# Long filter's rows by a transposing load through DRAM, slice 6's kv by four residues, a second buffer of turned h

## The chip, the cores and the metric

The kernel runs on one NeuronCore of a Trainium2 chip. The metric is the time of one execution in device microseconds; smaller is better. The engines are TensorE (PE; its weight loads are PEld), VectorE (DVE), ScalarE (ACT), GpSimd (POOL) and SyncE (SP). SP, ACT and POOL each have a queue from which they issue DMAs, in the order in which the instructions stand there.

## The reference

A forward pass and its gradients with respect to nine inputs, for a sequence of 2048 steps and 1024 channels:

```python
xn = _layernorm(q)
k_shift = sum over 4 taps of the shifted k * shift_k      # 4-tap causal filter per channel
kv = k_shift * v
y = irfft(rfft(kv padded to 4096) * rfft(ssm_k padded to 4096))[:2048]   # long convolution
s = xn * (y + kv * ssm_D)
g = silu(((xn @ w_gate) * (xn @ w_up)) @ w_down)          # 1024 -> 3584 -> 1024
out = q + s * g
```

The outputs are `out` and the gradients of q, k, v, shift_k, ssm_k, ssm_D, w_gate, w_up and w_down. `ssm_k` is stored with channels as rows (1024 x 2048): this is the long filter, called h in the kernel. The change touches how its rows get into the layout in which the convolution reads them.

## The kernel before, in words

**Work and stages.** The 1024 channels are cut into 8 slices of 128 (`ds`), the sequence into 16 blocks of 128 (`NB`), the hidden width 3584 into 14 slabs of 256 columns (`NSL`). The kernel goes through stages in one program: layer norm and the first gate/up units; gate/up matmuls of slabs 2 to 13 with the forward convolution woven in; the down projection with the gate; the gradients of h and of the weights with the backward convolution woven in; the gradient of x.

**Gate/up stage.** `gu_unit` takes a slab and a group of four sequence blocks: per block eight 512-column matmuls (L671) into a bank of `psg` (two banks), a copy out by ScalarE (L673) into `gut`, and per group a store of `gut` to GUd on ACT's queue. VectorE multiplies the two halves (hN); TensorE later turns hN (`turn`, `turn_pair`), ScalarE copies it to hT (L705, L724), and SP's queue stores hT to HTd. The slab's weights (wslab, two buffers) are loaded by SP's queue, so slab n+2 can be loaded when slab n is done with.

**Forward convolution.** `conv_forward` is a generator that does one slice after another. For a slice it transforms h (`kind` 1) and kv (`kind` 0) to 4096 frequencies, multiplies them, and transforms back. A forward transform does matmuls into `psF` (L234, two banks), copies by ScalarE into SP tiles, and butterflies on VectorE. Two forms exist: `fwd4_half` with four residues (32 matmuls of 256 columns for a slice, few VectorE sums) and `fwd8_half` with eight (16 matmuls, more VectorE sums). The list EIGHT names the (slice, kind) pairs that take eight.

**h's rows before the change.** `load_h` loads 128 rows of ssm_k into the first half of U[5] on POOL's queue. `h_rows(ds, c)` turns one half c of them on TensorE: eight 128x128 transposes (L786, L788) into a bank, and one scaled copy by ScalarE (L789) into `hx`. It is called twice per slice. The second half of U[5] serves as a third buffer of gut for slabs 0 to 11.

**What sets the order.** `make_pump` paces the generator: each gate/up block calls `tick`, which runs the generator until the sum of its yielded weights reaches a fraction of F_TOTAL; `net` takes planned TensorE time off each weight. Behind that, a scheduler orders the instructions of each engine and of each queue by when it reckons them ready, except those kept in program order (`keep_in_program_order`, used for conv matmuls and VectorE's instructions). A DMA on SP's or ACT's queue gets one of eight semaphores in turn, shared by the two queues, and waits until the DMA that had this semaphore before has landed.

**Taps.** The four taps of k's filter are laid out for all partitions in Wbc (8 KB a partition, whole kernel long), read by `shift` in the forward stage and by `dk_units` in the last.

Of the kernel before, what the change touches and what calls it, by code (L numbers as in the profile page):

```python
# [19 lines left out]
def build_kernel(  # L20
# [11 lines left out]
    nc = tc.nc  # L32
# [74 lines left out]
    HFd = dram.tile([8, P, 16, 256], BF16, name="HFd")  # L107
    KFd = dram.tile([8, P, 16, 256], BF16, name="KFd")
    DYFd = dram.tile([8, P, 16, 256], BF16, name="DYFd")
    GUd = dram.tile([NSL, 2, P, 2, 8, SLW], BF16, name="GUd")  # L110
    Hd = dram.tile([NSL, P, 2, NB, P], BF16, name="Hd")
    HTd = [[dram.tile([4, P, n, 256], BF16, name=f"HTd{i}{j}") for j, n in enumerate((8, 8, 8, 4))] for i in range(2)]
# [12 lines left out]
    nc.scalar.activation(warm[:], warm[:], ACT.Sqrt)  # L125
    RSTD = const.tile([P, NB], F32, name="RSTD")
    RSTN = const.tile([P, NB], F32, name="RSTN")
    Wbc = const.tile([P, 4, D], BF16, name="Wbc")

    tip = tc.alloc_tile_pool(name="tip", bufs=1)  # L130
    TI = tip.tile([P, 2, 8, 2, P], BF16, name="TI")
# [9 lines left out]
    def load_bcast(bsb):  # L141

        wrow = bsb.tile([1, D, 4], BF16, name="wrow")
        st(wrow[:].rearrange("p d j -> p (d j)"), A_shift_k.rearrange("(o d) j -> o (d j)", o=1))
        wtap = bsb.tile([1, 4, D], BF16, name="wtap")

        def turn(j):
            nc.gpsimd.tensor_copy(wtap[:, j, :], wrow[:, :, j])

        def spread():  # L150
            st(WTd.rearrange("(o x) -> o x", o=1), wtap[:].rearrange("p j d -> p (j d)"))
            st(Wbc[:].rearrange("p j d -> p (j d)"), bass.AP(WTd.tensor, WTd.offset, [[0, P], [1, 4 * D]]))
        return turn, spread

    def angles(tg):
# [87 lines left out]
    def net(w):  # L243
        w -= 0.95 * pe_us[0]
        pe_us[0] = 0.0
        return w

    def fwd4_half(x, i, wp, psp, first=None):

        pe_us[0] += 1.75  # L250
        SP = wp.tile([P, 2, 2, 512], F32, name="SP", bufs=2)
        for par in range(2):
            ps = psp.tile([P, 2, 2, 256], F32, name="psF")
            cmm(ps[:, 0], T4[par], x, (i, i + 4), first if i == 0 else None, True)
            cmm(ps[:, 1], T4[par], x, (i + 2, i + 6))
            nc.scalar.copy(out=SP[:, :, par], in_=ps[:].rearrange("p s k x -> p s (k x)"))
        return SP

    def fwd4_buf(wp):
# [27 lines left out]
    def fwd8_half(x, i, SP, psp, first=None, held=False):  # L287

        pe_us[0] += 0.87
        for j in range(2):  # L290
            r = 2 * i + j
            ps = psp.tile([P, 2, 2, 256], F32, name="psF")
            cmm(ps[:, 0], T4[0], x, (r,), first if r == 0 else None, held)
            cmm(ps[:, 1], T4[0], x, (r + 4,))
            nc.scalar.copy(out=SP[:, :, j], in_=ps[:].rearrange("p s k x -> p s (k x)"))  # L295

    def fwd8(SPs, X, W, C, ahead, late=False):

# [235 lines left out]
    Dz = kst.tile([P, D], BF16, name="Dz")  # L534
    V.memset(Dz[:], 0.0)
    krow = kst.tile([P, 2, 11, 256], BF16, name="k")
    V.memset(krow[0:1, 0, 0:3, :], 0.0)
    bsb = pool("bc_sb", 1)
    tg = pool("tg", 1)
# [115 lines left out]
    def gu_unit(sl, b0, n, w, tick):  # L655

        if n == 4:
            turn_of[0] += 1
            if turn_of[0] % 3 == 0 and sl < NSL - 2:
                gut = U[5][:, 2048:4096].rearrange("p (a i f) -> p a i f", a=2, i=4)  # L660
            else:
                gut = fg.tile([P, 2, 4, SLW], BF16, name="gut")
            hN = fg.tile([P, 2, 4, P], BF16, name="hN", bufs=3)
        else:
            gut = lnp.tile([P, 2, 2, SLW], BF16, name="gut_s", bufs=6)
            hN = lnp.tile([P, 2, 2, P], BF16, name="hN_s", bufs=6)
# [26 lines left out]
        hn[0] = multiply  # L693

        def turn_pair():
            hT = fg.tile([P, 4, 2, 2, P], BF16, name="hT", bufs=1)
            two_, mate[:] = mate[0:2], mate[2:]
            ps = tr_tile()[:].rearrange("p h b x -> p h (b x)").rearrange("p h (b u) -> p h b u", u=64)
            for qq in range(4):
                for a in range(2):  # L700
                    for i in range(2):
                        turn_halves(lambda hh: ps[:, hh, 4 * qq + 2 * a + i], two_[qq // 2][:, a, qq % 2 * 2 + i, :])
            to = HTd[b0 // 8][sl // 4][:, :, 2 * (sl % 4):2 * (sl % 4) + 2, :]
            for g in range(2):
                nc.scalar.copy(out=halves(hT[:, 2 * g:2 * g + 2].rearrange("p q a i s -> p (q a i) s")), in_=ps[:, :, 8 * g:8 * g + 8])  # L705
            ht_st[0] = ld(to.rearrange("q f a s -> f q (a s)"), hT[:].rearrange("f q a i s -> f q (a i s)"))

        def store(hT):
            half, rest = divmod(b0, 8)
# [5 lines left out]
                ht_st[0] = ld(to[q0, :, :, i0 * P:(i0 + n) * P], hT[:, 0, :, 0:n].rearrange("f a i s -> f a (i s)"))  # L715

        def turn():
            hT = fg.tile([P, 4, 2, 2, P], BF16, name="hT", bufs=1)[:, 0:2] if chunk[0] > 5 else lnp.tile([P, 2, 2, 2, P], BF16, name="hT_s", bufs=5)[:]
# [10 lines left out]
    h_out = []  # L729
    cv_gone = []  # L730
    ht_st = [None]
    EIGHT = ((0, 0), (0, 1), (6, 0), (7, 0), (7, 1))
    INV8 = (2, 4, 5, 6, 7)
    SHIFT_W = 8 * 2.3

# [4 lines left out]
    def conv_forward():  # L740
        S_ = conv_state

        def load_kv(dp, c):
            S_["k", dp] = krow
            if dp > 0 or c == 0:
                for i in range(2) if dp == 0 else (c,):
                    cld_k(krow[:, i], i, dp)
            if dp > 0 or c == 1:
                for i in range(2) if dp == 0 else (c,):
                    v = U[4][:, 2048 * i:2048 * i + 2048].rearrange("p (a x) -> p a x", a=8)  # L750
                    cld_v(v, i, dp * 256, 256)

        def load_h(ds):
            hrow = U[5][:, 0:2048].rearrange("p (c u r) -> p c u r", c=2, r=8)
            cld(U[5][:, 0:2048], A_ssm_k[ds * P:(ds + 1) * P, :])
            S_["h", ds] = hrow

        def shift(dp):
            kv = cx.tile([P, NB, 256], BF16, name="kv")
            S_["kvt", dp] = kv  # L760
            k = S_.pop(("k", dp))
            wb = lambda j: Wbc[:, j:j + 1, dp * 256:(dp + 1) * 256].unsqueeze(1).to_broadcast([P, 2, 8, 256])
# [12 lines left out]
            yield 2.3  # L775

        def h_rows(ds, c):
            if ds == 8:
                return
            hrow = S_["h", ds]  # L780
            if c == 0:
                S_["hx"] = cf.tile([P, NB, P], BF16, name="hx")
# [3 lines left out]
                nc.tensor.transpose(ps[:, 0, :], hrow[:, c, :, 0], ident[:])  # L786
            for r in range(1, 8):
                nc.tensor.transpose(ps[:, r, :], hrow[:, c, :, r], ident[:])  # L788
            nc.scalar.activation(S_["hx"][:, 8 * c:8 * c + 8, :], ps, ACT.Copy, scale=WSC)  # L789
            if c == 1:  # L790
                h_out.append(ds)
                if ds + 1 < 8:
                    load_h(ds + 1)

        def kvs(ds):
            return S_["kvt", ds // 2][:, :, ds % 2 * P:(ds % 2 + 1) * P]
# [70 lines left out]
        for ds in range(8):  # L867
            yield 0.5
            if ds % 2 == 1 and ds < 7:
                with tc.issue_after(S_["kst"].ins):  # L870
                    for c in range(2):
                        load_kv(ds // 2 + 1, c)
            D0 = Dz[:, ds * P:(ds + 1) * P]
            sph = []
            KX = cx.tile([P, 16, 256], BF16, name="KX")
# [5 lines left out]
            else:  # L881
                yield from transform(ds, 0, sp, KX, own_room(HX), lambda i: sph.append(half(ds, S_["hx"], i, D0)), nop)
                S_["kst"] = st(KFd[ds], KX[:])
            calls = []

            def behind():
                calls.append(0)
                if len(calls) % 2 == 0:
                    next(tl, None)
            room = cf.tile([P, 4, 256], F32, name="room", tag="hx")[:] if eight else None  # L890
            yield from transform(ds, int(ds > 0), sph, HX if ds else KX, room, nop1 if eight else lambda c: h_rows(ds + 1, c),
                                 behind)
            if ds == 0:
                S_["kst"] = st(KFd[0], KX[:])
            if eight:
                h_rows(ds + 1, 0)
            turned(HX, 1, 0, 1)
            yield 1.3
            if eight:
                h_rows(ds + 1, 1)  # L900
            if ds == 7:
                cf.release()
                S_["filters"] = False
# [43 lines left out]
    for i, (b0, n, x4) in enumerate(xs):  # L947
# [16 lines left out]
        if i == 4:  # L964
            with tc.issue_after(act_copy[0].ins):
                nc.scalar.activation(Dz[0:1, :], Dz[0:1, :], ACT.Copy, scale=WSC)
# [237 lines left out]
    def dk_units(ew):  # L1204
# [9 lines left out]
        def load_turned(i):  # L1214
# [7 lines left out]
                nc.sync.dma_start_transpose(out=dkT[:], in_=DKSHd[ds, c * H:c * H + H, :])  # L1222
            return kT, dkT

        dk = load_rows(0)
        yield 3
        for i in range(16):
            ds, c = divmod(i, 2)
            dsl = slice(ds * P, (ds + 1) * P)
            wb = lambda j: Wbc[:, j:j + 1, dsl].to_broadcast([P, 8, P])  # L1230
# [577 lines left out]
```

## Time and profile before

| | us |
|---|---|
| median of 3 runs (lowest, highest) | 1911.72 (1911.5, 1912.55) |
| the profiled execution | 1911.63 |
| its span, first to last instruction | 1909.9 |
| TensorE busy | 1899.4 |
| VectorE busy | 1549.7 |
| ScalarE busy | 636.8 |

The profile shows one execution. Busy time is the union of an engine's instructions; TensorE's matmuls overlap in their pipeline, so what a matmul costs is read from the start of one to the start of the next. A line of the timeline has start, duration, engine, line of the kernel, operation, output<-inputs, shapes and count, and in brackets an idle time before it with what ended it. "SPq", "ACTq" and "POOLq" are DMA issues on a queue; "to landing" is from the issue's start until the data has arrived. In the slice digits of the page the gate/up stage with the forward convolution is about the first 500 us.

### The profile page before, as it was taken

Reading aid. Unit: us, or ns where it says so; the run is one execution under the profiler, and the core shown is the slowest. Engines: PE = TensorE matmul, PEld = TensorE weight load, DVE = VectorE, ACT = ScalarE, POOL = GpSimd, SP = SyncE. Lnnn points to the kernel's source line nnn. Section 1 sums busy time; section 2 is a strip of 40 time slices with the busy share of each in tenths; the row PEclk is TensorE's granted clock in tenths of the full one; section 3 lists DMA queues with packets and bytes.
Section 4 is the critical chain, followed back from the end, with each engine's and each line's share of the span. In section 5 each row is a group of like instructions: output and inputs, shape, how many; then the busy total and the mean of one; then the engine's idle time right before and its main releaser. Section 6 shows DMA issues by size and latency. Waiting matters only on the chain.

```text
span 1909.9 us, 28150 instructions
## 1 busy us (share of the span) xinstructions
PE 1899.4 (99%) x11379; PEld 1013.9 (53%) x11379; DVE 1549.7 (81%) x1711; ACT 636.8 (33%) x927; POOL 332.7 (17%) x465
## 2 busy tenths in 40 slices
PE   8999999999999999999999999999999999999999
PEld 5555555545444466666666665664444444444444
DVE  8999999999988556887999999999995305788862
ACT  5765555556333233432222222222222102111121
POOL 5121211201113220001031221211212101111120
PEclk9999999999999999999999999999999999999999
DMA  9777766769769997677897798585887999989852
GB/s 298 269 263 233 251 208 223 252 211 311 241 227 307 316 314 231 209 231 233 264 277 247 231 266 258 184 286 180 230 238 181 219 206 190 194 187 190 194 166 88
DMA packets 425106, 444.34 MB, mean 233 GB/s; under 512 B 268400, under 2 KB 342796, under 8 KB 410512
## 3 DMA queue, kind: packets, MB, share of 16 engines
q1 hardware_dynamic: 367504, 239.03, 45.9%
q0 software_dynamic: 41152, 174.15, 29.0%
q10 hardware_dynamic: 16320, 29.36, 4.1%
q8 instruction: 89, 1.46, 0.3%
q14 instruction: 41, 0.34, 0.1%
HBM read 193.87 MB, written 189.84 MB: 201 GB/s over the span
## 4 chain that ended last, share of the span: by engine, by line
PE 97%; DVE 1%; ACT 1%; DMA 0%; issue 0%; SPq 0%; ACTq 0%
PE psb L1499 20%; PE psx L1644 20%; PE psg L671 19%; PE psb L1482 10%; PE psbm L1034 10%; PE psb L1582 9%; PE psF L234 3%; PE psI L455 1%; PE tr L565 1%; PE psY L1193 1%; PE psY L445 1%; PE psx L1582 1%; DVE bst L578 0%; DMA wslab<-in_B_w_gate_dram 0%; PE tr L788 0%; DVE U L212 0%
## 5 line engine op out<-in xcount | busy, mean ns | idle before, releaser
L671 PE MATMUL psg<-wslab,U 128*128 128x512 bf16 x1792 | 401.8, 379 | 3.5 <-DMA wslab<-in_B_w_gate_dram 2.1
L1499 PE MATMUL psb<-U,U 128*128 128x512 bf16 x1792 | 397.1, 379 | 0.0
L1644 PE MATMUL psx<-U,dgut 128*128 128x512 bf16 x1536 | 332.8, 379 | 0.0
L1644 PEld LDWEIGHTS <-dgut 128*128 128x128 bf16 x1792 | 175.3, 98 | 211.4
L1499 PEld LDWEIGHTS <-U 128*128 128x128 bf16 x1792 | 175.2, 98 | 198.0
L671 PEld LDWEIGHTS <-U 128*128 128x128 bf16 x1792 | 172.6, 98 | 197.2 <-issue 3.6
L1482 PE MATMUL psb<-wdt,U 128*128 128x256 bf16 x1792 | 205.6, 273 | 0.0
L1482 PEld LDWEIGHTS <-U 128*128 128x128 bf16 x1792 | 175.2, 98 | 29.2
L212 DVE TENSOR_TENSOR W<-W 128x1024 f32<-128x1024 f32 (+1 forms) x189 | 186.5, 1003 | 4.1
L1582 PE MATMUL psb<-U,U 128*128 128x512 bf16 x816 | 177.3, 379 | 0.0
L1504 ACT CAST wb<-psb 128x512 bf16<-128x512 f32 x112 | 65.6, 586 | 315.4 <-PE psb L1499 310.5
L1249 DVE SCALAR_TENSOR_TENSOR dkp<-dkT,kT 128x1024 bf16<-128x1024 bf16 (+2 forms) x64 | 78.3, 1223 | 93.1 <-DMA dkT<-DKSHd 91.4
L1034 PE MATMUL psbm<-U,ht 128*128 128x512 bf16 x672 | 146.0, 379 | 0.0
L1582 PEld LDWEIGHTS <-U 128*128 128x128 bf16 x896 | 87.4, 98 | 104.4
L673 ACT CAST gut<-psg 128x512 bf16<-128x512 f32 x156 | 91.5, 589 | 120.2 <-PE psg L671 119.7
L1676 ACT ACTIVATE dx_t<-dxn 128x1024 bf16<-128x1024 f32 x15 | 15.9, 1057 | 324.7 <-DVE dxn L212 324.7
L1034 PEld LDWEIGHTS <-ht 128*128 128x128 bf16 x672 | 65.7, 98 | 78.1
L212 DVE TENSOR_TENSOR U<-U,dht 128x2048 bf16<-128x2048 bf16 x56 | 68.3, 1220 | 46.5 <-ACT dht L1484 46.5
L1484 ACT CAST dht<-psb 128x512 bf16<-128x512 f32 x112 | 65.6, 587 | 116.4 <-PE psb L1482 116.4
L66 POOL DMA_DIRECT2D Hd<-hN x54 | 36.6, 677 | 268.9 <-DVE hN L212 258.9
L1623 ACT CAST wbs<-psb 128x512 bf16<-128x512 f32 x51 | 29.9, 586 | 145.4 <-PE psb L1582 134.3
L212 DVE TENSOR_TENSOR W<-SP 128x1024 f32<-128x1024 f32 x64 | 74.1, 1218 | 1.3 <-ACT SP L295 0.8
(263 smaller groups left out, 2342.9 us busy)
## 6 DMA issues: line engine op xcount, KB each, us to landing
U<-GUd SPq DMA_DIRECT2D x28, 1024.0 KB, 9.3
DGd<-U SPq DMA_DIRECT2D x28, 1024.0 KB, 5.8
GUd<-gut ACTq DMA_DIRECT2D x39, 512.0 KB, 5.2
out_dram<-wb SPq DMA_DIRECT2D x112, 128.0 KB, 4.8
U<-Hd SPq DMA_DIRECT2D x14, 1024.0 KB, 6.6
Hd<-hN POOLq DMA_DIRECT2D x54, 256.0 KB, 4.5
HTd<-hT SPq DMA_DIRECT2D x24, 512.0 KB, 3.7
ht<-HTd SPq DMA_DIRECT2D x18, 512.0 KB, 7.5
```

Of the source, the lines that this page charges most:

```text
L212: pinned(V.tensor_tensor(o, a, b, op))
L234: mm = nc.tensor.matmul(ps[:, k].rearrange("p (c d) -> p c d", c=2), T[:, r, k, :], xr[:, r], start=(n == 0), stop=(n == len(rs) - 1 and ( ...
L671: gu_mm[0] = nc.tensor.matmul(ps[:], XNT[q][:, dc, qi * P:(qi + 1) * P], w[:, dc].rearrange("p a f -> p (a f)"), start=(dc == 0), stop=(dc ...
L673: nc.scalar.copy(out=gut[:, :, i], in_=ps[:].rearrange("p (a f) -> p a f", a=2))
L1034: mm = nc.tensor.matmul(ps[:, dh * 512:(dh + 1) * 512], ht(fc)[:, i * P:(i + 1) * P], WD[fc // 4][:, fc % 4, dh * 512:(dh + 1) * 512], sta ...
L1249: ins = V.scalar_tensor_tensor(prod[:].rearrange("p r d -> p (r d)")[:, lo:H], dkT[:, 0, lo:H], 1.0, kT[:, 0, 13 + m + lo:13 + m + H], op0 ...
L1482: nc.tensor.matmul(ps[:, x * SLW:(x + 1) * SLW], DBMT[2 * hf + g][:, dc, (b % 4) * P:(b % 4 + 1) * P], wdt[:, dc, :], start=(dc == 0), sto ...
L1484: nc.scalar.copy(out=dht[:, 2 * e:2 * e + 2].rearrange("p b f -> p (b f)"), in_=ps[:])
L1499: nc.tensor.matmul(ps[:], XN[b // 4][:, b % 4, dc * P:(dc + 1) * P], dgus[b // 8][:, :, b % 8], start=(b == 0), stop=(b == NB - 1))
L1504: nc.scalar.copy(out=wb[:, dc % 2].rearrange("p a f -> p (a f)"), in_=ps[:])
L1582: nc.tensor.matmul(ps, h[:, f, b, :], DBM[b // 4][:, b % 4, dh * 512:(dh + 1) * 512], start=(b == 0), stop=(b == NB - 1))
L1644: nc.tensor.matmul(ps[:, dh * 512:(dh + 1) * 512], t[n][:, f, i * P:(i + 1) * P], WGU[n][:, f, dh * 512:(dh + 1) * 512], start=(n == 0 and ...
```

## The change

1. From slice 1 on, h's rows are turned by a transposing load on SP's queue (`turn_h`), straight from ssm_k into U[5]: the partition is then a step within a block of 128. `keep_h` stores that to HRd in DRAM in the order of the sequence (SP's queue), and `h_by_rows` loads it back into `hx` with eight consecutive steps to a partition (POOL's queue). Slice 0 keeps the TensorE way.
2. The scale WSC moves from h_rows' copy (and from Dz) into the copy of h's transform out of psF (`from_bank`).
3. (6, 0) leaves EIGHT.
4. Wbc is gone; 256-channel pieces of the taps are loaded into WB (two of them) and, in the last stage, wbk.
5. hT has two buffers; `turn_pair` stores it on ACT's queue; in slabs 12 and 13 half of krow is the third buffer of gut.
6. F_TOTAL is adapted.

```diff
-    Wbc = const.tile([P, 4, D], BF16, name="Wbc")
+    HRd = dram.tile([8, S, P], BF16, name="HRd")
+    WB = kst.tile([P, 4, 2, 256], BF16, name="WB")
...
+    def from_bank(out, ps, first):
+        if first is None:
+            nc.scalar.copy(out=out, in_=ps)
+        else:
+            nc.scalar.activation(out, ps, ACT.Copy, scale=WSC)
...
-            if turn_of[0] % 3 == 0 and sl < NSL - 2:
+            if turn_of[0] % 3 == 0 and sl >= NSL - 2:
+                gut = krow[:].rearrange("p a b d -> p (a b d)")[:, 2048:4096].rearrange("p (a i f) -> p a i f", a=2, i=4)
+            elif turn_of[0] % 3 == 0:
                 gut = U[5][:, 2048:4096].rearrange("p (a i f) -> p a i f", a=2, i=4)
...
         def turn_pair():
-            hT = fg.tile([P, 4, 2, 2, P], BF16, name="hT", bufs=1)
+            hT = fg.tile([P, 4, 2, 2, P], BF16, name="hT", bufs=2)
...
-            ht_st[0] = ld(to.rearrange("q f a s -> f q (a s)"), hT[:].rearrange("f q a i s -> f q (a i s)"))
+            ht_st[0] = sta(to.rearrange("q f a s -> f q (a s)"), hT[:].rearrange("f q a i s -> f q (a i s)"))
...
-    EIGHT = ((0, 0), (0, 1), (6, 0), (7, 0), (7, 1))
+    EIGHT = ((0, 0), (0, 1), (7, 0), (7, 1))
...
+        def turn_h(ds):
+            if ds < 8:
+                nc.sync.dma_start_transpose(out=U[5][:, 0:2048].rearrange("p (j d) -> p j d", d=P),
+                                            in_=A_ssm_k[ds * P:(ds + 1) * P, :])
+
+        def keep_h(ds):
+            if ds < 8:
+                ld(HRd[ds].rearrange("(j p) d -> p j d", p=P), U[5][:, 0:2048].rearrange("p (j d) -> p j d", d=P))
+
+        def h_by_rows(ds):
+            if ds < 8:
+                S_["hx"] = cf.tile([P, NB, P], BF16, name="hx")
+                cld(S_["hx"][:].rearrange("u (c r) d -> u c (r d)", c=2), HRd[ds].rearrange("(c u r) d -> u c (r d)", c=2, u=P))
+                h_out.append(ds)
...
         for ds in range(8):
             yield 0.5
...
+            turn_h(ds + 1)
...
+            keep_h(ds + 1)
...
-            yield from transform(ds, int(ds > 0), sph, HX if ds else KX, room, nop1 if eight else lambda c: h_rows(ds + 1, c),
-                                 behind)
+            yield from transform(ds, int(ds > 0), sph, HX if ds else KX, room, nop1, behind)
+            h_by_rows(ds + 1)
...
-            if eight:
-                h_rows(ds + 1, 0)
             turned(HX, 1, 0, 1)
             yield 1.3
-            if eight:
-                h_rows(ds + 1, 1)
...
+    F_TOTAL += 0.95 * 7 * 0.95
```

More of the change, by code (lines that the diff above doesn't have):

```diff
@@ L151, in spread @@
             st(WTd.rearrange("(o x) -> o x", o=1), wtap[:].rearrange("p j d -> p (j d)"))
-            st(Wbc[:].rearrange("p j d -> p (j d)"), bass.AP(WTd.tensor, WTd.offset, [[0, P], [1, 4 * D]]))
+            load_taps(WB[:].rearrange("p j e d -> p j (e d)"), 0, 512, ld)
         return turn, spread
@@ L255, in fwd4_half @@
             cmm(ps[:, 1], T4[par], x, (i + 2, i + 6))
-            nc.scalar.copy(out=SP[:, :, par], in_=ps[:].rearrange("p s k x -> p s (k x)"))
+            from_bank(SP[:, :, par], ps[:].rearrange("p s k x -> p s (k x)"), first)
         return SP
@@ L294, in fwd8_half @@
             cmm(ps[:, 1], T4[0], x, (r + 4,))
-            nc.scalar.copy(out=SP[:, :, j], in_=ps[:].rearrange("p s k x -> p s (k x)"))
+            from_bank(SP[:, :, j], ps[:].rearrange("p s k x -> p s (k x)"), first)
     def fwd8(SPs, X, W, C, ahead, late=False):
@@ L536, in build_kernel, with load_taps @@
     krow = kst.tile([P, 2, 11, 256], BF16, name="k")
+    WB = kst.tile([P, 4, 2, 256], BF16, name="WB")
+    def load_taps(t, d0, w, queue=st):
+        queue(t, bass.AP(WTd.tensor, WTd.offset + d0, [[0, P], [D, 4], [1, w]]))
     V.memset(krow[0:1, 0, 0:3, :], 0.0)
@@ L717, in turn @@
         def turn():
-            hT = fg.tile([P, 4, 2, 2, P], BF16, name="hT", bufs=1)[:, 0:2] if chunk[0] > 5 else lnp.tile([P, 2, 2, 2, P], BF16, name="hT_s", bufs=5)[:]
+            hT = fg.tile([P, 4, 2, 2, P], BF16, name="hT", bufs=2)[:, 0:2] if chunk[0] > 5 else lnp.tile([P, 2, 2, 2, P], BF16, name="hT_s", bufs=5)[:]
             ps = tr_tile()[:, 0].rearrange("p (q a i) x -> p q a i x", q=2, a=2)
@@ L744, in load_kv @@
             S_["k", dp] = krow
+            if dp > 1 and c == 0:
+                load_taps(WB[:, :, dp % 2], dp * 256, 256)
             if dp > 0 or c == 0:
@@ L753, in load_h @@
         def load_h(ds):
-            hrow = U[5][:, 0:2048].rearrange("p (c u r) -> p c u r", c=2, r=8)
             cld(U[5][:, 0:2048], A_ssm_k[ds * P:(ds + 1) * P, :])
-            S_["h", ds] = hrow
+            S_["h", ds] = U[5][:, 0:2048].rearrange("p (c u r) -> p c u r", c=2, r=8)
+        def turn_h(ds):
[10 more added lines that the diff above has]
+                h_out.append(ds)
         def shift(dp):
@@ L761, in shift @@
             k = S_.pop(("k", dp))
-            wb = lambda j: Wbc[:, j:j + 1, dp * 256:(dp + 1) * 256].unsqueeze(1).to_broadcast([P, 2, 8, 256])
+            wb = lambda j: WB[:, j:j + 1, dp % 2].unsqueeze(1).to_broadcast([P, 2, 8, 256])
             room = cx.tile([P, 16, 256], BF16, name="KX")[:].rearrange("p a x -> p (a x)") if dp == 0 else U[7][:]
@@ L777, in h_rows @@
         def h_rows(ds, c):
-            if ds == 8:
-                return
             hrow = S_["h", ds]
@@ L788, in h_rows @@
                 nc.tensor.transpose(ps[:, r, :], hrow[:, c, :, r], ident[:])
-            nc.scalar.activation(S_["hx"][:, 8 * c:8 * c + 8, :], ps, ACT.Copy, scale=WSC)
+            nc.scalar.copy(out=S_["hx"][:, 8 * c:8 * c + 8, :], in_=ps)
             if c == 1:
                 h_out.append(ds)
-                if ds + 1 < 8:
-                    load_h(ds + 1)
         def kvs(ds):
@@ L963, in build_kernel @@
                     next(conv)
-        if i == 4:
-            with tc.issue_after(act_copy[0].ins):
-                nc.scalar.activation(Dz[0:1, :], Dz[0:1, :], ACT.Copy, scale=WSC)
         for i_, sl in ([(0, 0)], [(1, 0), (0, 1), (1, 1)], [(2, 0), (2, 1)], [(3, 0), (3, 1)], [(4, 0)], [(5, 0)])[i]:
@@ L1223, in load_turned @@
             return kT, dkT
+        wbk = None
         dk = load_rows(0)
@@ L1229, in dk_units @@
             dsl = slice(ds * P, (ds + 1) * P)
-            wb = lambda j: Wbc[:, j:j + 1, dsl].to_broadcast([P, 8, P])
+            if i % 4 == 0:
+                wbk = ew.tile([P, 4, 256], BF16, name="wbk", bufs=2)
+                load_taps(wbk[:], ds * P, 256)
+            wb = lambda j: wbk[:, j:j + 1, ds % 2 * P:(ds % 2 + 1) * P].to_broadcast([P, 8, P])
             acc = ew.tile([P, 8, P], BF16, name="dka")
```

## The prediction

> **What bounds the kernel now.** I read the page's busy times and slices first, then the busy time by stage, then the waits of TensorE.
>
> ```profile
> span 1909.9 us, 28150 instructions
> PE 1899.4 (99%) x11379; PEld 1013.9 (53%) x11379; DVE 1549.7 (81%) x1711; ACT 636.8 (33%) x927; POOL 332.7 (17%) x465
> 110.00:160.00 50.00, 50.00 (x381) 28.31 (x378) 49.13 (x43) 29.30 (x40) 12.56 (x17) 1.00 0.85 275
> 160.00:300.00 140.00, 139.41 (x997) 74.73 (x996) 137.89 (x113) 76.31 (x106) 23.92 (x34) 1.00 0.70 231
> 300.00:420.00 120.00, 120.00 (x869) 64.79 (x867) 119.03 (x105) 67.71 (x94) 21.96 (x31) 1.00 0.72 238
> PE psg L671 <- ACT gut L673: 1.1, 2, 0.9
> PE psF L234 <- DVE kv L212: 0.6, 1, 0.6
> ```
>
> The stage rows give length, then busy time of PE, PEld, DVE, ACT, POOL, the granted clock, the DMA share and GB/s. TensorE never rests after the start; VectorE is 98 to 99% full from 110 to 420 us, so it has hardly any room; ScalarE is 55 to 59% busy. The granted clock is 1.00 throughout. The last two rows (waits of TensorE) show that TensorE waits for almost nothing. So a removed TensorE instruction shortens the kernel by its own time, and any hold of TensorE lengthens it by that hold: nothing later is idle that could take it up. The executed time beside this span is 1911.63 us, 0.1 under the median of the three runs (1911.72); I work from 1911.63.
>
> **What is removed and added on TensorE.** A block of h_rows (L786, L788) is eight transposes.
>
> ```profile
> 62.99 0.22 PE L786 MATMUL tr<-ident,U 128*128 128x128 bf16 x1
> 63.05 0.60 PE L788 MATMUL tr<-ident,U 128*128 128x128 bf16 x7
> 63.48 3.62 PE L671 MATMUL psg<-wslab,U 128*128 128x512 bf16 x16
> 120.28 1.91 PE L234 MATMUL psF<-kv,TF 128*128 128x256 bf16 x16
> 122.03 3.62 PE L671 MATMUL psg<-wslab,U 128*128 128x512 bf16 x16
> ```
>
> From the first transpose's start to the next matmul's start: 63.48 - 62.99 = 0.49 us. Slices 1 to 7 have two blocks each, so 14 x 0.49 = **6.9 us go**. Slice 6's kv loses its place in EIGHT: two halves of 16 matmuls instead of two of 8, 16 more. A half of 16 takes 122.03 - 120.28 = 1.75 us: **1.75 us come**. Net on TensorE -5.15 us. (By busy time a block is 0.22 + 0.60 us, which overlaps its neighbours; by that the net would be -9.7.)
>
> **VectorE.** The same edit spares VectorE work behind the four sums that both forms share.
>
> ```profile
> 75.92 1.22 DVE L212 TENSOR_TENSOR KX<-W 128x1024 f32<-128x1024 f32 x1
> 80.72 0.68 DVE L212 TENSOR_TENSOR hN<-gut 128x1024 bf16<-128x1024 bf16 x1
> 87.72 0.69 DVE L212 TENSOR_TENSOR hN<-U 128x1024 bf16<-128x1024 bf16 x1
> 134.45 4.62 DVE L212 TENSOR_TENSOR KX<-W 128x1024 bf16<-128x1024 f32 x4
> ```
>
> Eight residues: 87.72 - 75.92 less one hN of 0.6 = 11.2 us. Four residues: 4.6 us. So VectorE is spared 6.6 us in slice 6, more than TensorE's 5.15. The planner's total also moves: F_TOTAL gains 6.3 and loses 9.5, and each slice's weight grows by the 0.9 that h_rows used to subtract, so the convolution is spread over relatively more gate/up work. TensorE thus arrives at VectorE's results at about the same absolute time; I cost this at nothing, from -1 to +5 us (all TensorE gain before slice 6 lost at waits such as the kv one above).
>
> **Small things at nothing.**
>
> ```profile
> 106.64 1.02 ACT L789 ACTIVATE hx<-tr 128x1024 bf16<-128x1024 bf16 x1 [0.26 <-PE tr L788]
> 133.09 0.38 PE L234 MATMUL psF<-hx,TF 128*128 128x256 bf16 x2
> ```
>
> ScalarE drops 14 copies and has room. The scaling that h_rows did in its copy moves into copies that exist (from_bank). Slice loads of taps, hx from HRd and wbk go to POOL's queue, and each has several us to tens of us before its use: the old hx was ready at 107.7 us and first multiplied at 133.1, and a 512 KB load takes about 6 us (the in_A_ssm_k row below). Without that cover each hx would cost its landing, 6 us. The second buffer of hT, and krow as a third buffer of gut in slabs 12 and 13, can only take waits away, and no wait on them is in the list. Behind the stage, dk's work keeps the same VectorE operations.
>
> **What moves on the queues: the term that decides.** The order of the built program (each queue's instructions with the semaphore each waits for) shows what the diff does not. The scheduler has put all seven transposing loads early. On SP, behind slab 2's load, stand T1, HRd1, an HTd store, T2, HRd2, an HTd store, slab 3, T3, an HTd store, HRd3, T4, an HTd store, HRd4, T5, HRd5, T6, HRd6, slab 4, T7, HRd7, slab 5. U[5] has one buffer for them, so T and HRd alternate: each T waits for the HRd before it to land, each HRd for its T. That is one serial chain of DMAs.
>
> Nobody needs its data soon. But eight semaphores are handed round the DMAs of SP and ACT, and each DMA waits on its queue until the previous user of its semaphore has landed. In the new order ScalarE's stores inherit semaphores of the chain. By the store's time in the profile before: GUd at 91.13 us waits for HRd2, at 99.37 for slab 3, at 108.33 for HRd3, the HTd store behind the copy of 111.75 for T4, GUd at 115.92 for HRd4, **GUd at 124.57 for T6**, at 133.91 for HRd6, at 156.50 for T7. Behind a waiting store stand ScalarE's evictions of psg and psF; TensorE has two banks of each and then stops.
>
> ```profile
> 60.00:110.00 50.00, 49.79 (x316) 27.03 (x315) 48.84 (x56) 35.15 (x45) 8.04 (x12) 1.00 0.63 212
> 645.00:1185.00 540.00, 539.88 (x3401) 331.17 (x3400) 446.33 (x473) 166.52 (x258) 90.06 (x130) 1.00 0.83 254
> 91.13 0.52 ACTq L72 DMA_DIRECT2D GUd<-gut  x1
> 99.37 0.52 ACTq L72 DMA_DIRECT2D GUd<-gut  x1
> 108.33 0.52 ACTq L72 DMA_DIRECT2D GUd<-U  x1
> 111.75 1.93 ACT L705 COPY hT<-tr 128x1024 bf16<-128x1024 bf16 x2
> 115.92 0.52 ACTq L72 DMA_DIRECT2D GUd<-gut  x1
> 124.57 0.52 ACTq L72 DMA_DIRECT2D GUd<-gut  x1
> 125.69 0.58 ACT L673 CAST U<-psg 128x512 bf16<-128x512 f32 x1 [1.14 <-PE psg L671]
> 133.91 0.52 ACTq L72 DMA_DIRECT2D GUd<-U  x1
> 156.50 0.52 ACTq L72 DMA_DIRECT2D GUd<-gut  x1
> 66.99 0.60 PE L788 MATMUL tr<-ident,U 128*128 128x128 bf16 x7
> 127.23 1.89 PE L671 MATMUL psg<-wslab,U 128*128 128x512 bf16 x8
> 129.63 1.69 PE L671 MATMUL psg<-wslab,U 128*128 128x512 bf16 x7
> L1330 SPq DMA_TRANSPOSE wdt<-in_B_w_down_dram x14: 1700/4910/12837, 644.9 to 1185.4; - x14
> DMA to landing us min/median/max: 4.2/9.3/21.7
> U<-in_A_ssm_k_dram POOLq DMA_DIRECT2D x8, 512.0 KB, 6.0
> HTd<-hT SPq DMA_DIRECT2D x24, 512.0 KB, 3.7
> YFd<-yf POOLq DMA_DIRECT2D x7, 512.0 KB, 7.9
> wslab<-in_B_w_gate_dram SPq DMA_DIRECT2D x14, 512.0 KB, 9.2
> ```
>
> T1 can start when h_rows(0) is through, 66.99 + 0.60 = 67.6 us. A T has no row of its own. The nearest is wdt: the same 512 KB turned on the same queue, landing after 4.2 to 21.7 us, median 9.3; its stretch of the kernel (645 to 1185 us) has a DMA share of 0.83, this one 0.63 up to 110 us and 0.85 after. I take 9.3. HRd writes 512 KB in pieces of 256 B: between HTd<-hT (3.7, same queue, longer pieces) and YFd<-yf (7.9, the same pieces, POOL's queue); I take 4.5, nearer to the row of its own queue. Then HRd4 has landed at 67.6 + 4 x 13.8 = 122.8, T5 at 132.1, HRd5 at 136.6. By then ScalarE is held, its stores and POOL's have stopped, so T6 gets the quiet 4.2: **140.8 us**.
>
> Held at the store of 124.57, ScalarE cannot evict (125.69). TensorE still has the unit of 127.23 for its second bank and stops ahead of the unit of 129.63; having been spared two blocks by then, it stands there at 128.6. After T6 come the store's issue, 0.52, and one eviction, 0.58: TensorE goes on at 141.9. **Hold: 13.3 us.** Everything behind it shifts by as much, so HRd6 (145.3 against 133.91 + 12.3), slab 4 (140.9 + 9.2 = 150) and T7 (154.6 against 156.5 + 12.3) come in time.
>
> Bounds of this term: with 4.2 and 3.7 throughout T6 lands at 67.6 + 6 x 4.2 + 5 x 3.7 = 111.3 and there is no hold; with 12 (inside wdt's upper half) and 5.8 it lands at 168.6 and the hold is 41.
>
> **Sum:** 1911.63 - 6.9 + 1.75 + 13.3 = **1919.8 us**, 0.4% slower.
>
> **A rule that speaks against this hold.** The Trainium skill, "Advanced Engine Details and Errata", section "X-Bar Transpose (TRN2)", states that transposing DMAs are as fast as regular ones. By it T would take the 6.0 us of the plain load of the same rows, HRd4 would land at 109.6, T6 at 67.6 + 6 x 6.0 + 5 x 4.5 = 126.1, and the sum would be the first rival's 1906.5. The trace only half agrees: wdt's quickest, 4.2, is below 6.0, its median of 9.3 well above.
>
> **Rivals.**
> 1. The chain is quick enough (faster). If T and HRd together take under 10.9 us (T6 landed by 127.5: 59.9 us for five and a half pairs), TensorE is not held: 1911.63 - 5.15 = 1906.5. For it: no one waits for the data, wdt's quiet 4.2, and the plain load's 6.0. Against: ScalarE's and POOL's stores and slab 3 share the DMA engines, and six landings in a row have to be good.
> 2. A short hold, or VectorE (no change). T6 between 129 and 136 us costs 1.5 to 9 us and eats the 5.15; or no hold comes, but VectorE, with 1 to 2% room, is where TensorE's time goes until slice 6, as at the 0.6 us wait for kv: 1908 to 1915. For it: VectorE's 98 to 99%. Against: the planner's shift and the 6.6 us spared.
> 3. A longer hold. At 12 and 5.8 us a pair the hold is 41 us, 1948; at wdt's 11 and HRd's 5 it is 67.6 + 66 + 25 - 127.5 = 31, 1938. For it: wdt's 21.7, and that from 110 us on the DMA engines are at 0.85 without the chain. Against: the hold itself stops the other traffic.
> 4. The change does not do what it says, because the loads come too late for hx. The order excludes it: all seven stand before slab 5.
>
> **How the numbers follow.** About 0.2% (3.8 us) is what a measurement of this kernel tells from no change. The forecast and the longer hold (rival 3) share the condition that T6 lands after 136.5: 0.58 together, of which the longer hold beyond 1934 is 0.08. Rival 1 has 0.24, rival 2 has 0.18. So faster 0.24, same 0.18, slower 0.58. The range reaches from rival 1's 1906 to 1934 (a hold of 27 us, T at 10.5 and HRd at 4.7), leaving out about 0.18.
>
> **What would show it.** TensorE transposes of L814 and its neighbour: 16 left. The hold: an idle time of PE psg of some ten us between 118 and 145 us, released by ScalarE's eviction, with GUd stores on ACT's queue at the landing of a transposing load; SP's queue with T and HRd in turn, T6 landing near 141. If T6 lands before 127.5 and PE has no such gap, rival 1 holds and my term is wrong in T's duration. If psF waits for kv or for the sums on VectorE between 160 and 420, it is rival 2. If the gaps sit elsewhere, at the hx loads or the slabs, my reading of the queues is wrong.

## The result and the profile after

The changed kernel takes **1944.82 us** (median of five, 1938.17 to 1947.98) against 1911.86 before (1911.5 to 1912.55): ratio **1.0169, 95% interval 1.0151 to 1.0187**. It is slower, as forecast, and by stores held behind the chain, as forecast, but by 33 us where 8 were expected; the time lies outside the range of 1906 to 1934. The profiled execution of the changed kernel is the quickest of the five, 1938.17 us (span 1936.4), so the trace below explains 26.5 us of span and not the 6.7 us by which the median is longer still.

First the page and TensorE's waits of the changed kernel (who waits for whom: us in total, times, longest).

```profile
span 1936.4 us, 27939 instructions
PE 1899.1 (98%) x11283; PEld 1009.3 (52%) x11283; DVE 1543.7 (80%) x1699; ACT 622.9 (32%) x912; POOL 337.6 (17%) x470
PE psg L683 <- ACT gut L685: 15.7, 5, 9.3
PE psg L683 <- ACT U L685: 12.3, 1, 12.3
```

TensorE now waits 15.7 + 12.3 = 28.0 us for ScalarE's evictions of psg; before, the first of these rows said 1.1. ScalarE's own timeline shows why: the stores on its queue (ACTq), with the eviction behind each.

```profile
120.27 0.54 ACTq L72 DMA_DIRECT2D GUd<-U  x1
120.93 1.07 ACT L685 CAST gut<-psg 128x512 bf16<-128x512 f32 x2 [12.11 <-DMA HRd<-U]
...
126.71 0.45 ACTq L72 DMA_DIRECT2D HTd<-hT  x1
...
132.50 0.55 ACTq L72 DMA_DIRECT2D GUd<-gut  x1
...
157.60 0.52 ACTq L72 DMA_DIRECT2D GUd<-gut  x1
158.24 0.58 ACT L685 CAST U<-psg 128x512 bf16<-128x512 f32 x1 [16.78 <-DMA U<-in_A_ssm_k_dram]
```

And the chain of waits of the same stretch (start, us, what): the transposing loads T and the stores HRd, one behind the other.

```profile
93.80 11.20 DMA U<-in_A_ssm_k_dram
105.01 15.18 DMA HRd<-U
120.21 6.42 DMA U<-in_A_ssm_k_dram
126.69 5.73 DMA HRd<-U
132.44 16.79 DMA U<-in_A_ssm_k_dram
149.24 3.82 DMA HRd<-U
153.08 4.45 DMA U<-in_A_ssm_k_dram
...
158.87 7.05 PE psg L683 x24
...
174.91 3.45 PE psg L683 x16
```

These are T3, HRd3, T4, HRd4, T5, HRd5, T6. Each store of ScalarE leaves at a landing of the chain: GUd at 120.27 behind HRd3 (120.2), HTd at 126.71 behind T4, GUd at 132.50 behind HRd4, GUd at 157.60 behind T6 (157.5). TensorE's timeline has a gap behind three of them (9.34, 3.58 and 12.26 us).

```profile
121.57 8.66 PE L683 MATMUL psg<-wslab,U 128*128 128x512 bf16 x32 [9.34 <-ACT gut L685]
133.81 2.38 PE L683 MATMUL psg<-wslab,U 128*128 128x512 bf16 x8 [3.58 <-ACT gut L685]
135.97 3.14 PE L234 MATMUL psF<-kv,TF 128*128 128x256 bf16 x16
142.40 1.91 PE L234 MATMUL psF<-kv,TF 128*128 128x256 bf16 x16
144.15 1.89 PE L683 MATMUL psg<-wslab,U 128*128 128x512 bf16 x8
158.87 6.40 PE L683 MATMUL psg<-wslab,U 128*128 128x512 bf16 x21 [12.26 <-ACT U L685]
```

Two of these rows show something else: the same 16 matmuls of psF take 3.14 us behind a gap and 1.91 us later. The table by stretch (length, then busy time of PE, PEld, DVE, ACT, POOL, the granted clock, DMA share, GB/s) says why.

```profile
100.00:120.00 20.00, 12.22 (x98) 6.21 (x97) 16.41 (x19) 4.69 (x6) 5.38 (x8) 0.86 1.02 298
120.00:130.00 10.00, 8.43 (x32) 3.48 (x32) 2.19 (x3) 4.08 (x6) 1.20 (x2) 0.76 0.72 193
150.00:160.00 10.00, 1.13 (x3) 0.40 (x3) 0.00 (x0) 1.76 (x3) 0.00 (x0) 0.50 0.66 144
160.00:165.00 5.00, 5.00 (x19) 2.06 (x18) 2.51 (x3) 4.05 (x6) 0.00 (x0) 0.76 0.99 262
```

The column before the last two is the granted clock: it falls with the gaps, to 0.50. What that costs: the 24 matmuls of 158.87 took 7.05 us, at 3.45 / 16 = 0.216 us each they take 5.2, so 1.9; the 32 of 121.57 at 0.216 plus the 0.2 that such a row counts at its end take 7.1, so 1.6; the 8 of 133.81 lose 2.38 - 1.89 = 0.5; psF loses 3.14 - 1.91 = 1.2. Together 5.2 us. The account of the profiled run closes: 28.0 - 1.1 of waits, + 5.2 of clock, - 5.15 saved on TensorE = 26.95, and the span grew by 26.5; the other waits of TensorE differ by under 1 us each.

The Trainium skill, "TensorE: Matmul & The Clock Gate", Part 1, says that TensorE falls to half its clock after an idle window of about 3.4 us and needs as long busy to leave it. The trace agrees on the half, 0.50, and about on the way back: in windows of half a us the clock is at 1.00 again 3.3 and 3.5 us after TensorE went on at 121.57 and 158.87. It fell sooner, 2.4 and 2.1 us into these two gaps.

### The profile page after: what moved, and what is told of

It reads as the page before. It is cut to its first block, busy times and chain, and to the rows that moved or that the text cites. A ratio compares the mean times of both kernels' runs of the same rounds, so it can differ in the third digit from the quotient of the medians.

```text
span 1936.4 us, 27939 instructions
## 1 busy us (share of the span) xinstructions
PE 1899.1 (98%) x11283; PEld 1009.3 (52%) x11283; DVE 1543.7 (80%) x1699; ACT 622.9 (32%) x912; POOL 337.6 (17%) x470
## 4 chain that ended last, share of the span: by engine, by line
PE 93%; DMA 5%; DVE 1%; ACT 0%; SPq 0%; issue 0%; ACTq 0%
PE psb L1523 20%; PE psx L1668 20%; PE psg L683 17%; PE psb L1506 10%; PE psbm L1054 10%; PE psb L1606 9%; PE psF L234 3%; DMA U<-in_A_ssm_k_dram 3%; DMA HRd<-U 2%; PE psI L461 1%; PE psY L1213 1%; PE tr L575 1%; PE psY L451 1%; PE psx L1606 1%; DVE bst L588 0%; DMA wslab<-in_B_w_gate_dram 0%
## 5 line engine op out<-in xcount | busy, mean ns | idle before, releaser
L683 PE MATMUL psg<-wslab,U 128*128 128x512 bf16 x1792 | 405.4, 382 | 30.4 <-ACT gut L685 15.7
L685 ACT CAST gut<-psg 128x512 bf16<-128x512 f32 x144 | 84.1, 589 | 133.3 <-PE psg L683 115.3
```

The costliest lines, as they stand in the source:

```text
L683: gu_mm[0] = nc.tensor.matmul(ps[:], XNT[q][:, dc, qi * P:(qi + 1) * P], w[:, dc].rearrange("p a f -> p (a f)"), start=(dc == 0), stop=(dc ...
L685: nc.scalar.copy(out=gut[:, :, i], in_=ps[:].rearrange("p (a f) -> p a f", a=2))
```

## The experiments

Theory 1 (the prediction's): ScalarE's stores wait for semaphores of the chain, and the evictions stand behind them. Rival A: VectorE takes the gain. Rival B: the chain's traffic itself slows TensorE's data wherever it stands. Rival C: another part of the change. "Leaves out" in an expectation tells which part of the computation is missing. The kernel before, run beside them, took 1911.85 to 1912.22 us at the median. In two kernels one execution stands far off (5204 us in the seventh, 1999 in the eighth) and nothing here explains these two; the table leaves them out.

| kernel | median us | range | ratio to before, 95% |
|---|---|---|---|
| 1 T paced by the slab loads | 1918.42 | 1911.8-1927.6 | 1.0023-1.0051 |
| 2 no chain | 1910.02 | 1906.6-1913.9 | 0.9984-1.0001 |
| 3 T without HRd | 1920.91 | 1917.8-1928.8 | 1.0039-1.0066 |
| 4 ScalarE's stores on POOL's queue | 1935.75 | 1933.1-1942.1 | 1.0116-1.0143 |
| 5 plain loads in place of T | 1920.98 | 1919.4-1923.3 | 1.0035-1.0061 |
| 6 HRd in long pieces | 1942.40 | 1938.0-1945.2 | 1.0144-1.0170 |
| 7 k and v of slices 2, 3 cut | 1927.50 | 1926.9-1929.5 | 1.0067-1.0102 |
| 8 no chain, taps early | 1914.11 | 1906.6-1919.2 | 0.9996-1.0019 |
| 9 before, (6,0) alone | 1914.07 | 1913.7-1915.4 | 0.9998-1.0015 |
| 10 no chain, HTd on SP | 1908.90 | 1906.2-1916.4 | 0.9971-0.9994 |
| 12 paced, stores on POOL | 1914.09 | 1909.3-1919.1 | 0.9996-1.0016 |

**1. Pacing.**

```
+        slab_new[0] = last            # in load_slab
+            with tc.issue_after(slab_new[0].ins):
                 nc.sync.dma_start_transpose(...)
```

> The changed kernel, but each transposing load of turn_h is set to be issued behind the newest slab load, so that on SP's queue the seven T stand one or two to a slab (T1 behind slab 2, T2 behind slab 3, T3 behind slab 5 and so on) instead of all ahead of slab 5. All data are computed as in the changed kernel. Theory (ScalarE is held because its stores wait for semaphores of a packed chain of T and HRd): no store of ScalarE waits for a T or HRd under way, the two long idle times of PE psg near 120 and 150 us are gone, the granted clock stays at 1.00, and the time is 1911.9 - 6.9 + 1.75 = 1906.7 us (1905.5 to 1909). Rival A (VectorE binds until slice 6, so the spared transposes are lost at its results): 1909 to 1912. Rival B (the transposing loads' traffic itself slows TensorE or the slabs, wherever they stand): above 1925.

1918.42 us, 26 less than the changed kernel with the same transfers: most of the loss is where T stands, not that it runs. But it is 12 above the 1906.7 expected, so theory 1 is not the whole. The profiled execution took 1913.22 us, so its trace can show only the first 6.5 us of these 12. It has one long wait in the stage, in the timelines of TensorE and ScalarE; the last row is from the median landings between 55 and 420 us.

```profile
291.24 2.29 PE L686 MATMUL psg<-wslab,U 128*128 128x512 bf16 x5 [5.43 <-ACT U L688]
267.94 0.52 ACTq L72 DMA_DIRECT2D GUd<-U  x1
290.60 1.07 ACT L688 CAST U<-psg 128x512 bf16<-128x512 f32 x2 [8.20 <-DMA GUd<-U]
U<-in_A_ssm_k_dram SPq DMA_TRANSPOSE x7, 12.9
```

A GUd store issued at 267.94, 7 us behind a T, landed at 290.5, and the eviction that needs its buffer came late. Here ScalarE waits for a store of its own to land, not for a borrowed semaphore; that much of rival B is real. The same store in the kernel without the chain (experiment 2), issued at 268.05, landed in 7.0 us.

**2. The ceiling.** turn_h and keep_h are not called; hx is loaded from in_A_ssm_k, unturned.

> The changed kernel without the transposing loads and without the stores to HRd; hx of slices 1 to 7 is loaded in the same piece size (2 KB) straight from in_A_ssm_k, unturned, so the turning of slices 1 to 7 is left out of the computation. It is the ceiling: all that the change does on TensorE, VectorE and ScalarE, without the chain. Theory: 1911.9 - 5.15 = 1906.7 us (1905.5 to 1909), no idle time of PE psg over 1 us. Rival A (VectorE takes the gain): 1909 to 1912. Rival C (the slow-down is not the chain but something else of the change, such as the taps loaded by slice, the moved HTd stores or the loads of hx): above 1925.

1910.02 us: no 28 us of waits, so the loss is the chain's (rival C falls as to size). The time would fit rival A, but the profile doesn't: its one wait on VectorE in the stage is 0.3 us, and the largest is far behind it.

```profile
PE psx L1666 <- ACT wbs L1645: 3.1, 1, 3.1
PE psF L234 <- DVE kv L212: 0.3, 1, 0.3
```

1909.9 - 5.15 + 3.1 = 1907.9, against a span of 1908.2: TensorE did gain its 5.15, and a wait in the last stage took most of it back. That this wait comes and goes would fit the range of 1906.6 to 1913.9, but one execution was profiled, so it is not shown.

**3. T alone.** keep_h is not called; T stays; hx is loaded as in kernel 2.

> As the kernel without the chain, but the seven transposing loads are kept (nobody uses their data; the stores to HRd are left out, and hx is loaded unturned, so the ordering of the rows of slices 1 to 7 is left out of the computation). The T stand early and close together on SP's queue; ScalarE's GUd store of 91 us now waits for T5 and that of 108 us for slab 3. Theory: the hold depends on what a store of ScalarE waits for, so TensorE stands once, ahead of 110 us, until T5 has landed: T1 at 67.6, five times some 8 us, so till about 108: a hold of 5 to 15 us, and 1912 to 1922 in all. If the T are as quick as the plain load of the same rows (6 us) T5 lands at 98 and the time is 1907 to 1910: then HRd alone makes the loss. If a transposing load is slowed by whatever runs beside it to 12 or more, it is above 1925 without any HRd.

The hold moved to the store that waits for T5, as the order says (ScalarE's and TensorE's timelines):

```profile
100.20 0.54 ACTq L72 DMA_DIRECT2D GUd<-gut  x1
100.78 1.86 ACT L193 COPY TI<-psT 128x2048 bf16<-128x2048 bf16 x1 [9.39 <-DMA U<-in_A_ssm_k_dram]
103.19 8.40 PE L683 MATMUL psg<-wslab,U 128*128 128x512 bf16 x31 [7.63 <-ACT gut L685]
```

T1 to T5 ran from 67.9 to 100.2, one in 6.5 us: with no HRd between them T is near a plain load's 6.0. (T7, issued at 111.1, took 20.5, with no HRd in this kernel at all; SP's next load of slab 4 left at 131.58, when T7 landed.) A hold of 7.6 us in another place, behind another link, is what theory 1 foretold and rivals A, B and C did not.

**4. The stores off ScalarE's queue.** sta issues on POOL's queue.

> The changed kernel with the GUd and HTd stores that ScalarE issues (sta) put on POOL's queue; the packed chain of T and HRd stays early on SP. All data are computed. Theory (the loss is ScalarE's evictions standing behind stores that wait for the chain): ScalarE no longer stands behind a waiting store; TensorE goes on through 115 to 160 us, except for what a late slab 4 (still behind T6 on SP) or POOL's own queue costs; 1907 to 1920. Rival B (the traffic of the chain itself, or data that come late because of it): PE psg still idles about 28 us and the time stays at 1935 to 1948.

A miss: 1935.75, where theory 1 gave 1907 to 1920. ScalarE no longer holds TensorE as it did, but the chain's other victim comes forward (SP's and TensorE's timelines):

```profile
144.75 4.41 SPq L773 DMA_TRANSPOSE U<-in_A_ssm_k_dram  x1
156.94 3.24 SPq L557 DMA_DIRECT2D wslab<-in_B_w_up_dram  x1
174.77 12.77 PE L683 MATMUL psg<-wslab,U 128*128 128x512 bf16 x47 [12.43 <-DMA wslab<-in_B_w_gate_dram]
```

Slab 4 stands behind T6 and HRd6 on SP's queue, goes out at 156.94 and keeps TensorE 12.43 us. (A further gap, 4.67 us ahead of 138.99, stands behind a copy of ScalarE that waited 5.66 us for a store of HTd to land.) So theory 1 has to be widened: the chain packed early delays **everything queued behind it or sharing its semaphores**, and freeing one victim lets the next set the end.

**5, 6, 7. What made the chain long.**

```
5 -  nc.sync.dma_start_transpose(out=U[5]..., in_=A_ssm_k[...])
  +  ld(U[5][:, 0:2048], A_ssm_k[ds * P:(ds + 1) * P, :])
6 -  ld(HRd[ds].rearrange("(j p) d -> p j d", p=P), ...)
  +  ld(HRd[ds].rearrange("(p j) d -> p (j d)", p=P), U[5][:, 0:2048])
7 k: t[u:u+n, a:] -> t[u:u+n, a:a+1]; v: a:a+4 -> a:a+1, for slices 2 and 3
```

> The changed kernel with each transposing load T replaced by a plain load of the same 512 KB on the same queue and at the same place, so that the chain of load, HRd, load, HRd keeps its order and the stores of ScalarE that wait for it stay the same (the turning of slices 1 to 7 is left out of the computation). If the transposing form is what makes the chain long (9.0 us in the mean for T1 to T6): the plain load takes about 6.0, HRd 4.5 to 6, the sixth load lands at 126 to 134 and the time is 1907 to 1918. If the chain is slow because any transfer beside so much traffic is (HRd in plain pieces took 15.2 us once): loads of 8 to 9 us, the sixth landing at 145 to 158, and 1928 to 1948.

> The changed kernel with HRd stored in one piece of 4 KB a partition instead of 16 of 256 B (the rows of slices 1 to 7 are then not put in order; that part of the computation is left out). The scheduler puts T7 ahead of slab 4 too here. If HRd's 7.2 us in the mean comes from its short pieces: HRd about 3.7, T6 lands near 140, and with the hold some 15 us shorter 1920 to 1930. If HRd waits for the traffic beside it whatever its pieces are: the sum stays at 1935 to 1950.

> The changed kernel in which the loads of k and v for slices 2 and 3 (2.4 MB on POOL's queue, issued at 110 to 133 us in the changed kernel) fetch one row of each piece only; everything else, the order of each queue and the waits included, is as in the changed kernel (the filter of slices 2 and 3 is computed from stale rows). Theory (the chain stretched in the hold because POOL's loads, already issued, shared the DMA engines with it: HRd3 15.2 and T5 16.8 us): HRd3 about 7 and T5 about 9, T6 lands near 141 instead of 157.5, the idle time of PE psg is 12 to 15 us instead of 28, and the time is 1919 to 1926, near the 1919.8 of the prediction. Rival (the transposing load itself is that slow at times, or KFd's and HFd's stores do it): 1935 to 1948.

With plain loads the sixth landed at 139.2 and the time is 1920.98, between the two answers: the kernel is 24 us quicker without the transposing form. From the start of each load to the start of its HRd, the six took 7.5, 3.8, 8.1, 4.3, 5.5 and 3.8 us; T1 to T6 in the changed kernel 8.2, 6.9, 11.2, 6.4, 16.8 and 4.4. But a plain store was stretched as well (SP's queue, kernel 5; HRd4, and the load that waits for its landing):

```profile
106.27 0.36 SPq L61 DMA_DIRECT2D HRd<-U  x1
126.09 0.34 SPq L61 DMA_DIRECT2D U<-in_A_ssm_k_dram  x1
127.45 3.53 PE L683 MATMUL psg<-wslab,U 128*128 128x512 bf16 x8 [9.64 <-ACT gut L685]
```

HRd4 took 19.8 us there. Long pieces shorten HRd (mean of the first five 4.9 us for 7.2) and change nothing in all: T4 and T6 then took 16.4 and 18.9, and T6 landed at 154.2. With k and v cut the time is 1927.50, between the two answers and 17 under the changed kernel. The transposing form is kept here, so the 24 of kernel 5 and these 17 are not shares of one sum. T5 and T6 took 5.7 and 5.4, with neither k nor v beside them: what is left of these loads also went out earlier in that kernel, at 110.8 to 122.7 us. T4 still took 19.2 (chain of waits, kernel 7):

```profile
106.82 19.20 DMA U<-in_A_ssm_k_dram
126.08 5.49 DMA HRd<-U
131.59 5.73 DMA U<-in_A_ssm_k_dram
137.33 3.81 DMA HRd<-U
141.16 5.40 DMA U<-in_A_ssm_k_dram
```

So there are two crowded places. From 105 to 125 us whatever link is under way takes 15 to 20 us, in either form and either direction: HRd3 15.2 (changed kernel), HRd4 19.8 (5), T4 16.4 (6), T4 19.2 (7). Kernel 7 shows that whole k and v are not needed for it; that it is KFd, HFd, the slab and the GUd stores that crowd it was not tried by itself. From 129 us on, in the changed kernel, it is v and k: T5 16.8 beside them, 5.7 without. Kernel 6 bears this out: v and k went out at 135 to 140 us there and met T6, which took 18.9.

The two forms differ in what goes on beside the stretched link. Beside T4 of kernel 6, KFd and HFd landed in 16.4 and 19.4 us; beside the plain HRd4 of kernel 5 in 6.6 and 9.1. (In kernel 7, without k and v, they took 9.5 and 13.2 beside T4.)

**8, 9, 10. The small parts.** Kernel 8 loads wbk three steps ahead in kernel 2; 9 is the kernel before with (6, 0) out of EIGHT; 10 is kernel 2 with turn_pair's ld in place of sta.

> The kernel without the chain, with the taps of the next two slices (wbk, in the stage behind the forward convolution) loaded three steps ahead of their use rather than at it (the turning of slices 1 to 7 is left out of the computation as there). Theory (the 3 us that the kernel without the chain lies above 1906.7, and its spread of 7 us, come from wbk's loads, for which VectorE waits 30.7 us in all and which shift the loads and stores behind): 1905.5 to 1908 with a spread under 3 us. Rival (they come from elsewhere in the change): 1909 to 1912 again.

> The kernel before with one part of the change alone: slice 6's kv by four residues, that is (6, 0) out of EIGHT. All data are computed. Theory (TensorE sets the end, so 16 more matmuls in two halves cost 1.75 us, and VectorE's 6.6 us spared bring nothing): 1911.9 + 1.75 = 1913.6 us (1912.8 to 1914.6). Rival (VectorE binds ahead of slice 6, so that its spared time shortens the kernel): 1907 to 1911. Rival (nothing either way): 1911.5 to 1912.5.

> The kernel without the chain (no transposing loads, no HRd; hx of slices 1 to 7 loaded unturned, so their turning is left out of the computation), with turn_pair's stores of HTd on SP's queue again, as in the kernel before, rather than on ScalarE's. Theory (the 3 us that the kernel without the chain lay above 1906.7, and its spread of 1906.6 to 1913.9, come from the HTd stores standing in ScalarE's order): 1905.5 to 1908, spread under 2 us as before the change. Rival (they come from the remaining parts, the loads of hx in pieces of 2 KB on POOL's queue, the third gut buffer or the taps): 1909 to 1912 with the same spread.

Kernel 9 came out at the theory: + 1.85 us on the median beside it (the interval just includes no change), VectorE's busy time down from 1549.7 to 1544.6 us, and nothing gained by that. Kernels 8 and 10 did not settle the spread: 8 was no better than 2; 10's median is 1.1 lower than 2's, its spread no smaller. The kernel before, run beside 9 and 10, itself had four of 23 executions between 1914.7 and 1919.2 us, so such a spread is not the change's alone. In 10's profile the waits lie in the last stage again:

```profile
PE psx L1666 <- DVE dxn L212: 4.6, 1, 4.6
```

Which transfer makes that stage late in some executions stays open.

**12. Both victims freed.** Kernel 1 with kernel 4's edit.

> The paced kernel (each transposing load behind the newest slab load) with ScalarE's GUd and HTd stores put on POOL's queue as well. All data are computed. It removes both holds shown so far: no slab load stands behind the chain, and ScalarE issues no store that could wait for a T. What is left of the paced kernel's 1918.4 us (and its spread of 16 us) above 1906.7 to 1910 is told by it. If it came from stores of ScalarE that still wait for a paced T's semaphore (five do by the built order): 1906 to 1911. If it is the transfers themselves, slowed beside a T (GUd landing in 22.6 us, T in 12.9 at the median and 30 at most), so that buffers come free late: 1914 to 1925, with PE psg waiting for ScalarE's evictions that wait for GUd's landing.

1914.09, just inside the second answer: 4 above the kernel without the chain, with the same late buffer in TensorE's and ScalarE's views. It is 4.3 under kernel 1; that this part was stores waiting for a paced T would fit, but kernel 1's profile shows no such wait, so it is not shown.

```profile
292.04 15.07 PE L686 MATMUL psg<-wslab,U 128*128 128x512 bf16 x56 [4.36 <-ACT U L688]
ACT U L688 <- DMA GUd<-U: 7.1, 1, 7.1
```

None of the kernels that compute everything beats the kernel before: even without any chain only some 2 to 3 us are to be had at the median (kernels 2 and 10; kernel 8 was 2 us slower than the kernel before).

## Why the prediction was right or wrong

- **What bounds the kernel** held: each us of hold on TensorE came out in the time.
- **-6.9 + 1.75** held: kernel 9 has + 1.85 for the second term; kernels 2, 8 and 10 reach 1906.2 to 1906.6 in their best executions, against 1906.5. Their medians are 2 to 8 us higher; the profiles of 2 and 10 show waits in the last stage (3.1 and 4.6 us); "small things at nothing" was too kind there.
- **VectorE** (a half of rival 2) is excluded: spared 5.1 us of busy time by (6, 0) against 6.6 worked out, it gave nothing (kernel 9), and without the chain TensorE waited 0.3 us for it in the stage (kernel 2).
- **The order on the queues** held link by link: the stores left at HRd3, T4, HRd4 and T6, as listed. The prediction told the delay as one stop, since HRd3 was to land at 67.6 + 3 x 13.8 = 109.0, 0.7 behind its store at 108.33 and within what two banks cover; it landed at 120.2 and cost the first gap, 9.34 us. That alone does not change the sum: the term of 13.3 us counts from 128.6, where TensorE was to stand, to 141.9, where it was to go on behind T6, and holds whatever was lost on the way. So it is not to be compared with the last gap alone, 12.26 us.
- **The step that failed is the size of the hold, 13.3 us**, through the durations of T and HRd. TensorE went on at 158.87, so the term measured 158.87 - 128.6 = 30.3 us: the gaps, and 3.3 us of slower matmuls behind the first two of the three long ones. T6 landed at 157.5 for 140.8, and these 16.7 us are nearly all of the miss. "I take 4.5" for HRd: the first five took 6.7, 4.4, 15.2, 5.7 and 3.8, mean 7.2. "I take 9.3" for T was fair in the mean (9.0), but T5 took 16.8. "By then ScalarE is held, its stores and POOL's have stopped" was wrong for T5: POOL's queue had issued v and k between 129 and 133 us, and in kernel 7, with neither beside it, it took 5.7. T6 did get its quiet time (4.45 for 4.2). Of the 16.7 us HRd3 is 10.7, T5 7.5, the other HRd 2.6, the other T and what lay before T1 -4.1. What crowded HRd3 stays open.
- The first excess could have been read in the profile before. The medians came from the whole kernel; the window of 105 to 120 us there has slab 3 landing at two to three times its medians there (6.6 and 9.2 us):

```profile
wslab<-in_B_w_up_dram SPq DMA_DIRECT2D x1, 512.0 KB, 19.0
wslab<-in_B_w_gate_dram SPq DMA_DIRECT2D x1, 512.0 KB, 20.3
```

  The second could not: from 132 to 150 us that profile is quiet (landings of 4.3 to 5.6 us). It was the hold itself that put v and k there: they went out at 118.1 to 122.5 us before and at 129.4 to 133.8 after, since POOL's queue stood at an Hd store until 128.8, VectorE's hN for it having waited 9.04 us for ScalarE's gut.
- **The clock** behind the gaps was left out: 5.2 us, of which 3.3 lie within the delay above and 1.9 come on top. With both the prediction's sum is 1911.63 - 5.15 + 30.3 + 1.9 = 1938.7, against 1938.17 for the profiled execution; the further 6.7 us of the median no trace shows.
- **Rival 3** (the longer hold) is what happened; its "against", that the hold stops the other traffic, is the claim that fell. **Rival 1** fell with the durations. **Rival 4** fell as argued: TensorE's list has no wait for hx. The rule quoted ahead of the rivals from the Trainium skill, "Advanced Engine Details and Errata", section "X-Bar Transpose (TRN2)", that transposing DMAs are as fast as regular ones, does not hold beside this traffic: kernel 5 differs from the changed kernel in that form, and in which link two of the stores wait for, and is 24 us quicker. (The two stores that bind in it leave at HRd4 and T6, as in the changed kernel.) It nearly held where T followed T (6.5 us against 6.0, kernel 3).

## What to carry to other kernels

Price a chain of transfers by the landings in the very window where it will run, link by link, and add up who is crowded there; a median over the kernel hides the bursts. Ask too what the hold itself will move into that window. When a scheduler may hoist loads that nobody needs soon, list every queue and every reused semaphore behind them: freeing one victim (ScalarE's stores) only hands the wait to the next (the slab). A hold of TensorE costs more than its length, since the matmuls behind it run at a lower clock for some us.

## What the runs showed of the hardware that was not expected

- After gaps of 3.6 to 12.3 us TensorE ran for some us at a lower granted clock, 0.50 in the stretch that ends the longest gap; about 5.2 us here on 25 us of gaps.
- Beside a transposing load other transfers landed late. In the paced kernel T's median landing rose to 12.9 us; beside the T issued at 260.65, which took 30.1, a 512 KB GUd store landed in 22.6 us, and HFd and YFd in 22.7 and 24.2. In the kernel without the chain the same three took 7.0, 6.2 and 8.0. The first row is the paced kernel's store, the second that of the kernel without the chain (both from the DMA view of 267 to 269 us), the third the median in the stage of the kernel before:

```profile
GUd<-U ACTq DMA_DIRECT2D x1, 512.0 KB, 22.6
GUd<-U ACTq DMA_DIRECT2D x1, 512.0 KB, 7.0
GUd<-U ACTq DMA_DIRECT2D x14, 512.0 KB, 6.5
```

- The piece length of HRd (256 B or 4 KB) made no difference to the time: 1942.40 against 1944.82 us.
